# A spectral token mixer followed by an ELU feed-forward: the first two quads of the feed-forward with the plain eight block products, and the opening ordered anew

## The chip, the cores and the metric

The kernel runs on one NeuronCore of one Trainium2 chip, and the figure is the device time of one execution in microseconds. All arithmetic is in float32. Lower is better.

## The reference

```python
X = np.fft.rfft(x, axis=1)                      # x: (8, 3008, 256)
Y = X * (filt_r + 1j * filt_i)[None]            # filters: (1505, 256)
y = np.fft.irfft(Y, n=3008, axis=1)
t = y.reshape(24064, 256)
h = t @ w_in                                    # w_in: (256, 2048)
g = np.where(h > 0, h, np.exp(np.minimum(h, 0)) - 1)
out = (g @ w_out).astype(np.float32)            # w_out: (2048, 256)
```

The feed-forward's weights come as float64: the kernel converts each of them on the chip from its two 32-bit words.

## The kernel before

**The feed-forward.** It is the bulk. The 8 batches b are cut into 6 groups of tokens m (448 tokens in m = 0, 512 in the others), and the 2048 hidden units into 4 parts q. A **quad** is one (b, m, q); there are 192, and TensorE goes through them one after another. In each quad both layers are 2 x 2 block matrices, multiplied with Winograd's seven products instead of eight: `up_steps` gives seven products per quad for the first layer, `down_steps` seven for the second, and the downs of quad i-1 stand between the ups of quad i in a pattern of U and D. A product is two matrix multiplications, and the profile shows it as four records of 128x224 or 128x256.

The seven products need sums: of the weights (`w_sums`, four additions for each half layer, kept as slices 4 to 6 of `w_in[q]`, `w_out[q]` and in place in slice 1), of the tokens (`n_sums`, and in the first group four subtractions at the end of `n_first`), of the hidden units (four subtractions in the tail of `up_steps`) and of the results (seven additions, in `down_steps`' tail, `c_unit` and `c_last`). ScalarE copies products out of PSUM and does Relu and Exp of the ELU; VectorE joins the products and does the ELU's maximum.

**The order.** The kernel writes each engine's instructions in the order in which they are to run (`tc.manual_schedule`): engines take them in order, and a wait holds up all that stands behind it on that engine. Work that is not a product is placed by hand: `at(quad, place, fn, ...)` puts a step at one of five places in a quad (2, 4, 0, 3, 1 in order of time), and the list `early` holds the weights' and the first batches' steps of quads 0 to 9. Items 2 to 5 of the quads are (0, 1, 0..3), and the rest of group (0, 0) comes as items 6 and 7. So (0, 0) is summed in two parts: the result of its first two quads is kept in `part` and added by `c_part` in quad 9.

**The opening.** Before quad 0 batch 0 goes through the mixer on its own path: `x_load_first`, `a_first` (six of them), `t_first`, and for eight groups of frequencies `b_first`, `products` (four VectorE multiplications each, two sets per group) and `bi_first`, then `y_write_first`, `y_read_first` and `n_first`. Nine `warm` multiplications stand between the last `bi_first` and `n_first`. Weights are fetched in 16 pieces k (`w_fetch`, from SP's queue), and each is converted by `w_split` (VectorE, two instructions), `w_float` (ScalarE, three), `w_join` (VectorE, two) and `w_mult` (VectorE or GpSimd); pieces 0, 1 are `w_in[0]`, 2, 3 `w_out[0]`, 4, 5 `w_in[1]`, 6, 7 `w_out[1]`, and so on. `OPEN` places these among the groups. From quad 2 on, `a_unit`, `b_unit`, `bi_unit` and `n_unit` carry the mixer of batches 1 to 7 between the products; `x_unit` (VectorE or, by `XPOOL`, GpSimd) prepares their input.

Of the kernel before, what the change touches and what calls it, by code (L numbers as in the profile page):

```python
# [37 lines left out]
XPOOL = ((1, 1), (0, 0), (0, 1), (0, 1), (1, 1), (0, 0))  # L38
WTMP = (0, 1, 0, 1, 0, 2, 3, 1, 0, 3, 3, 2, 3, 2, 3, 2)
# [107 lines left out]
def kernel(  # L147
# [338 lines left out]
    def b_unit(b, g):  # L486
# [96 lines left out]
    def half(m):  # L583

        return 224 if m == 0 else 256
# [23 lines left out]
    def n_first(w):  # L609

        h = half(0)
        (y0, y1, s) = ysets[0]
# [10 lines left out]
        b11, b12, b21, b22 = b1[:, 0], b1[:, 1], b2[:, 0], b2[:, 1]  # L623
        t1, t2, t4 = (s[:, i, 0:h] for i in range(3))
# [109 lines left out]

    PLACE = {1: (0, 0), 5: (0, 1), 3: (1, 0), 7: (1, 1), 2: (2, 0), 6: (2, 1), 4: (3, 0)}

    def down_steps(b, m, q):
        h = half(m)
        g = g_of.pop((b, m, q))
        begin, last = q == 0 or (b, m, q) == (0, 0, 2), q == 3 or (b, m, q) == (0, 0, 1)  # L740
# [16 lines left out]
        def tail():  # L757
# [4 lines left out]
            if q == 1:  # L762
                c = part
            else:
                c = kp.tile([P, 2, 512], FP32, tag="c", name="c")
# [155 lines left out]
    with tc.manual_schedule():  # L921


        with tc.tile_pool(name="boot", bufs=1) as bp:
# [22 lines left out]
            for k in range(4):  # L947
                nc.tensor.matmul(warm, t2[:, 0, 0, 0:P], t2[:, 0, 0:2].rearrange("p u d -> p (u d)"), start=True, stop=True)
# [6 lines left out]
            x_load_first(1)  # L955
            nc.sync.dma_start(once, once_d)
            nc.sync.dma_start(gs[:, 1:3], gs_d[:, 1:3])
            x_load_first(0)
            x_load_first(2)
            x_load_first(3)  # L960
            x_load_first(5)
# [21 lines left out]
            f_read_first(2, 4, 0, nc.sync)  # L983
            f_read_first(2, 4, 1, nc.gpsimd)
# [6 lines left out]
            OPEN = {4: ((w_split, 1),),  # L991
                    6: ((w_float, 1, 1),),
                    7: ((tn_read, 0, 1), (w_split, 0), (w_float, 1, 2),),
                    8: ((w_float, 0, 1), (w_float, 1, 0),),
                    9: ((w_float, 0, 0), (w_join, 0, 1), (w_join, 1, 0, 1), (w_mult, 1, nc.vector),),
                    10: ((w_fetch, 3, nc.sync), (w_float, 0, 2),),
                    11: ((w_join, 0, 0), (w_mult, 0, nc.vector), (w_fetch, 5, nc.sync),),
                    12: ((w_split, 2), (w_float, 2, 0, 1), (w_join, 2, 1), (w_fetch, 4, nc.sync), (w_float, 2, 2), (w_join, 2, 0),),
                    13: ((w_mult, 2, nc.gpsimd), (w_split, 4), (w_split, 3), (w_sums, 1, nc.gpsimd),),
                    14: ((w_fetch, 6, nc.sync), (w_float, 3, 1),),  # L1000
                    15: ((w_fetch, 7, nc.sync), (w_float, 4, 1), (w_float, 3, 0),),
                    16: ((w_float, 3, 2), (w_float, 4, 0), (w_join, 3, 0), (w_join, 4, 1),),
                    17: ((w_split, 6), (w_float, 6, 0), (w_join, 6, 1), (w_float, 6, 1, 2), (w_float, 4, 2), (w_join, 3, 1), (w_join, 6, 0), (w_mult, 6, nc.gpsimd), (w_fetch, 9, nc.sync), (w_split, 5), (w_split, 9), (w_join, 4, 0),),
                    18: ((w_float, 5, 0), (w_fetch, 8, nc.sync), (w_mult, 3, nc.vector), (w_join, 5, 1), (w_float, 5, 1), (w_split, 7), (w_float, 9, 1),),
                    19: ((w_float, 5, 2), (y_write_first, 4, 8, 24), (w_mult, 4, nc.gpsimd),)}
# [6 lines left out]
            a_first(0)  # L1012
            a_first(1)
            conv(1)
            conv(2)
            a_first(2)
            conv(3)
            conv(4)
            a_first(3)
            conv(5)  # L1020
            a_first(4)
            conv(6)
            a_first(5)
# [41 lines left out]
        def at(quad, place, fn, *a):  # L1065
# [3 lines left out]
        early = ((0, 2, w_sums, 3, nc.gpsimd), (0, 2, y_read, 0, 1), (0, 2, w_fetch, 11, nc.sync), (0, 2, y_write_first, 0, 8, 24), (0, 2, w_float, 7, 0), (0, 2, w_join, 5, 0), (0, 2, x_load, 1, 1), (0, 2, w_float, 9, 0),  # L1069
                 (0, 4, w_float, 7, 1), (0, 4, w_split, 8), (0, 4, w_join, 7, 1), (0, 4, w_float, 7, 2),  # L1070
                 (0, 0, w_join, 7, 0),
                 (0, 3, w_fetch, 10, nc.sync), (0, 3, w_mult, 7, nc.gpsimd), (0, 3, w_mult, 5, nc.gpsimd), (0, 3, y_write_first, 2, 8, 24), (0, 3, w_fetch, 12, nc.sync), (0, 3, x_load, 1, 0), (0, 3, w_float, 8, 1),
                 (0, 1, w_float, 8, 2), (0, 1, w_sums, 5, nc.gpsimd), (0, 1, y_write_first, 6, 8, 24), (0, 1, y_write_first, 3, 8, 24),
                 (1, 2, w_float, 8, 0), (1, 2, w_split, 11), (1, 2, x_unit, 1, 0, 0),
                 (1, 4, n_unit, 0, 1), (1, 4, w_fetch, 15, nc.sync), (1, 4, w_float, 9, 2),
                 (1, 0, y_write_first, 5, 8, 24), (1, 0, x_unit, 1, 1, 0), (1, 0, w_join, 9, 1), (1, 0, x_unit, 1, 1, 1), (1, 0, w_sums, 7, nc.gpsimd), (1, 0, n_sums, 0, 1, 0, 1), (1, 0, w_join, 8, 1),
                 (1, 3, w_float, 11, 0), (1, 3, n_sums, 0, 1, 2), (1, 3, w_float, 11, 1),
                 (1, 1, w_join, 8, 0), (1, 1, w_mult, 8, nc.gpsimd),
                 (2, 4, w_float, 11, 2), (2, 4, w_join, 9, 0), (2, 4, w_join, 11, 0), (2, 4, w_mult, 9, nc.gpsimd),
                 (2, 0, x_unit, 1, 0, 1), (2, 0, w_sums, 9, nc.gpsimd), (2, 0, w_fetch, 14, nc.sync),  # L1080
                 (2, 3, w_split, 10), (2, 3, w_float, 10, 0),
                 (2, 1, w_float, 10, 1, 2), (2, 1, w_join, 10, 0), (2, 1, w_join, 11, 1), (2, 1, x_load, 1, 3), (2, 1, x_load, 1, 2), (2, 1, f_arrange, 1, 1),
                 (3, 2, c_unit, 0, 0),
                 (3, 4, x_unit, 1, 2, 0), (3, 4, w_fetch, 13, nc.sync), (3, 4, w_mult, 11, nc.gpsimd), (3, 4, w_join, 10, 1), (3, 4, x_unit, 1, 3, 0),
                 (3, 0, w_mult, 10, nc.gpsimd), (3, 0, x_unit, 1, 3, 1), (3, 0, w_split, 12),
                 (3, 3, f_arrange, 0, 0), (3, 3, w_float, 12, 1), (3, 3, y_write_first, 1, 8, 24),
                 (3, 1, x_unit, 1, 2, 1),
                 (4, 2, w_float, 12, 2), (4, 2, y_write_first, 7, 8, 24), (4, 2, w_split, 13), (4, 2, f_arrange, 0, 1), (4, 2, w_float, 12, 0),
                 (4, 4, w_float, 13, 1), (4, 4, w_join, 12, 1), (4, 4, x_unit, 1, 4, 0), (4, 4, w_float, 13, 0), (4, 4, x_unit, 1, 5, 0), (4, 4, w_float, 13, 2),
                 (4, 0, w_join, 13, 1), (4, 0, x_unit, 1, 5, 1), (4, 0, f_arrange, 1, 0), (4, 0, x_unit, 1, 4, 1), (4, 0, w_join, 13, 0), (4, 0, w_join, 12, 0), (4, 0, tn_read, 0, 2),  # L1090
                 (4, 3, y_read, 0, 2), (4, 3, w_mult, 12, nc.gpsimd),
                 (4, 1, w_mult, 13, nc.gpsimd), (4, 1, w_sums, 11, nc.gpsimd), (4, 1, w_sums, 13, nc.gpsimd), (4, 1, w_split, 14),
                 (5, 2, w_split, 15),
                 (5, 4, c_last, 0, 0), (5, 4, w_float, 14, 0), (5, 4, w_float, 15, 0), (5, 4, w_float, 14, 1), (5, 4, w_float, 15, 1), (5, 4, w_join, 15, 1), (5, 4, w_float, 14, 2), (5, 4, w_float, 15, 2),
                 (5, 0, w_join, 14, 1), (5, 0, w_join, 15, 0),
                 (5, 3, w_join, 14, 0), (5, 3, w_mult, 15, nc.gpsimd), (5, 3, w_mult, 14, nc.vector),
                 (5, 1, w_sums, 15, nc.gpsimd),
                 (6, 2, n_unit, 0, 2), (6, 2, y_read, 0, 3),
                 (6, 0, n_sums, 0, 2, 0, 1), (6, 0, tn_read, 0, 3),
                 (7, 2, n_sums, 0, 2, 2),  # L1100
# [60 lines left out]
        items = [(b, m, q) for b in range(B) for m in range(6) for q in range(4)]  # L1161
        items[2:8] = items[4:8] + items[2:4]
        for i in range(-PER, len(items) + 3):
            ups, up_tail = up_steps(*items[i]) if 0 <= i < len(items) else ((), None)
            downs, down_tail = down_steps(*items[i - 1]) if 1 <= i <= len(items) else ((), None)
            ups, downs = list(ups), list(downs)
            for n, k in enumerate("DUUDUDDU" if i in opens else "UUDUDDU"):
# [53 lines left out]
```

## Time and profile before

| | us |
|---|---|
| median of 3 runs (2542.19 to 2544.31) | 2542.7 |
| profiled execution, own time | 2540.18 |
| its span in the profile | 2538.1 |
| TensorE busy (share of the span) | 2513.2 (99%) |
| VectorE busy | 2106.5 (83%) |
| ScalarE busy | 1528.9 (60%) |
| GpSimd busy | 158.1 (6%) |
| mean granted TensorE clock | 0.998 |

The span begins with the first instruction and ends with the last; the own time has some 2 us around it. Times of single steps below are counted from the span's start. Matrix multiplications are pipelined, so neighbouring records overlap, and a record is longer than the distance to the next.

### The profile page before, as it was taken

What the parts mean: (1) busy time and instruction counts of PE and PEld (TensorE: products, weight loads), DVE (VectorE), ACT (ScalarE), POOL (GpSimd) and SP (SyncE); (2) the same over time, 40 slices, a digit from 0 to 9 for tenths busy, and PEclk for the clock granted to TensorE, in tenths of its full rate; (3) what the DMA queues carried; (4) which work ended last, traced back from release to release, by engine and by line L of the source; (5) the groups of instructions that cost most, each with busy time, mean ns of one, the idle gap of its engine ahead of it and who ended that gap; (6) DMA issues with size and microseconds to landing.
All of it is one profiled execution on the core that took longest, in us unless ns stands there. A gap on an engine that the chain in (4) does not pass through costs nothing.

```text
span 2538.1 us, 43881 instructions
## 1 busy us (share of the span) xinstructions
PE 2513.2 (99%) x16748; PEld 2140.8 (84%) x16748; DVE 2106.5 (83%) x3667; ACT 1528.9 (60%) x2706; POOL 158.1 (6%) x229
## 2 busy tenths in 40 slices
PE   9999999999999999999999999999999999999998
PEld 5787789888898888888889888888889888898887
DVE  6998998888988889798887888878887788866766
ACT  6665666655566555656566656666555565555554
POOL 3531000000000000000000000000000010000000
PEclk9999999999999999999999999999999999999999
DMA  7744445323243322433234322333223032220010
GB/s 207 204 112 100 104 99 130 76 58 90 60 99 80 70 65 55 104 65 78 63 82 112 69 58 59 74 84 71 57 47 84 21 69 50 54 46 18 13 24 17
DMA packets 224929, 192.08 MB, mean 76 GB/s; under 512 B 125221, under 2 KB 205639, under 8 KB 221983
## 3 DMA queue, kind: packets, MB, share of 16 engines
q1 hardware_dynamic: 213791, 165.44, 27.7%
q0 software_dynamic: 9776, 23.58, 4.6%
q8 instruction: 132, 2.16, 0.4%
q14 instruction: 78, 0.64, 0.1%
q10 hardware_dynamic: 1152, 0.26, 0.1%
HBM read 117.33 MB, written 74.97 MB: 76 GB/s over the span
## 4 chain that ended last, share of the span: by engine, by line
PE 93%; DVE 3%; DMA 1%; SPq 1%; ACT 1%; issue 1%; DVEq 0%; ACTq 0%
PE po L750 44%; PE phs L667 25%; PE phd L667 12%; PE pha L667 6%; PE pso L595 2%; PE pv L560 1%; PE pf L494 1%; PE psa L296 1%; PE pse L595 0%; DMA xc<-in_x_dram 0%; DVE g L675 0%; DMA x<-in_x_dram 0%; DVE g L689 0%; SPq L816 0%; PE po L381 0%
## 5 line engine op out<-in xcount | busy, mean ns | idle before, releaser
L750 PE MATMUL po<-g,wo 128*128 128x256 f32 (+1 forms) x5376 | 1316.3, 377 | 0.0
L750 PEld LDWEIGHTS po<-g,wo 128*128 128x128 f32 x5376 | 1013.9, 190 | 169.9 <-issue 50.6
L678 ACT ACTIVATE g<-phs 128x512 f32<-128x512 f32 (+1 forms) x576 | 339.1, 589 | 686.3 <-PE phs L667 685.8
L667 PE MATMUL phs<-y,wi 128*128 128x256 f32 (+1 forms) x2288 | 580.9, 376 | 2.4 <-ACT g L678 1.4
L685 ACT ACTIVATE e<-e 128x512 f32<-128x512 f32 (+1 forms) x768 | 477.2, 621 | 24.3
L667 PEld LDWEIGHTS phs<-y,wi 128*128 128x128 f32 x2288 | 429.4, 190 | 60.3 <-ACT g L678 3.9
L675 DVE TENSOR_TENSOR g<-phd,g 128x512 f32<-128x512 f32 (+1 forms) x384 | 258.2, 672 | 231.6 <-ACT e L685 141.3
L684 ACT ACTIVATE e<-g 128x512 f32<-128x512 f32 (+1 forms) x576 | 353.3, 613 | 68.0 <-DVE g L675 57.3
L689 DVE SCALAR_TENSOR_TENSOR g<-e,g 128x512 f32<-128x512 f32 (+1 forms) x576 | 392.6, 682 | 0.8 <-ACT e L685 0.7
L689 DVE SCALAR_TENSOR_TENSOR g<-e,phs 128x512 f32<-128x512 f32 (+1 forms) x192 | 129.7, 676 | 116.0 <-ACT e L685 115.7
L667 PE MATMUL phs<-ys,wi 128*128 128x256 f32 (+1 forms) x784 | 200.2, 378 | 5.7 <-ACT g L678 2.6
L667 PE MATMUL phd<-y,wi 128*128 128x256 f32 (+1 forms) x768 | 195.6, 377 | 4.2 <-DVE g L675 4.2
L667 PE MATMUL phd<-ys,wi 128*128 128x256 f32 (+1 forms) x768 | 194.0, 375 | 0.8 <-DVE g L675 0.7
L667 PE MATMUL pha<-ys,wi 128*128 128x256 f32 (+1 forms) x752 | 190.0, 375 | 0.0
L684 ACT ACTIVATE e<-phs 128x512 f32<-128x512 f32 (+1 forms) x192 | 113.0, 588 | 114.2 <-PE phs L667 113.6
L667 PEld LDWEIGHTS phs<-ys,wi 128*128 128x128 f32 x784 | 147.4, 191 | 24.2 <-POOL wi L904 2.2
L667 PEld LDWEIGHTS phd<-y,wi 128*128 128x128 f32 x768 | 145.1, 191 | 24.1 <-DVE g L675 7.6
L667 PEld LDWEIGHTS phd<-ys,wi 128*128 128x128 f32 x768 | 145.7, 190 | 18.1 <-DVE g L675 1.8
L667 PEld LDWEIGHTS pha<-ys,wi 128*128 128x128 f32 x752 | 142.9, 190 | 16.4
L675 DVE TENSOR_TENSOR g<-pha,g 128x512 f32<-128x512 f32 (+1 forms) x192 | 129.0, 672 | 19.1 <-PE pha L667 15.8
L726 DVE TENSOR_TENSOR g<-g,g 128x512 f32<-128x512 f32 (+1 forms) x192 | 131.9, 687 | 6.7
L729 DVE TENSOR_TENSOR g<-g,g 128x512 f32<-128x512 f32 (+1 forms) x192 | 131.1, 683 | 6.7
(210 smaller groups left out, 2081.5 us busy)
## 6 DMA issues: line engine op xcount, KB each, us to landing
t<-yd SPq DMA_DIRECT2D x94, 256.0 KB
fall<-fp POOLq DMA_DIRECT2D x112, 192.0 KB, 5.2
t<-z SPq DMA_DIRECT2D x112, 192.0 KB
yd<-t SPq DMA_DIRECT2D x112, 192.0 KB
out_dram<-o SPq DMA_DIRECT2D x632, 32.0 KB
xc<-in_x_dram SPq DMA_DIRECT2D x153, 128.0 KB
z<-t SPq DMA_DIRECT2D x144, 128.0 KB
tn<-tn_t SPq DMA_DIRECT2D x47, 128.0 KB
```

The lines of the kernel that those rows point to most:

```text
L296: nc.tensor.matmul(p[32 * o:32 * o + 32, :, :], w[r, ts(o, 32)], x_part(t, o % 2, o // 2)[r], start=True, stop=True, tile_position=(32 * a ...
L494: nc.tensor.matmul(pf[p][1][32 * a:32 * a + 32, js, :], fb[r, v, :], t2[r, js, a, :], start=True, stop=True, tile_position=(32 * p, 32 * a))
L595: nc.tensor.matmul(p[o:o + 64, dh, ds(64 * q, n)], t[r, i - 4 * m, ds(dh * P + o, 64)], w[r, i - 4 * m, 0:n], start=True, stop=True)
L667: nc.tensor.matmul(ps[:, a, 0:h], w_in[q][:, COMBO[n], a, :], y[n], start=start and a == 0, stop=True, skip_group_check=True)
L675: nc.vector.tensor_tensor(out=g[o], in0=i0, in1=i1, op=ALU.add)
L678: nc.scalar.activation(out=g[o], in_=i0, func=AXT.Copy)
L684: nc.scalar.activation(out=e, in_=src, func=AXT.Relu, scale=-1.0)
L685: nc.scalar.activation(out=e, in_=e, func=AXT.Exp, scale=-1.0)
L689: nc.vector.scalar_tensor_tensor(out=g[n], in0=es[n], scalar=1.0, in1=src, op0=ALU.subtract, op1=ALU.max)
L726: nc.vector.tensor_tensor(out=b12, in0=b22, in1=b12, op=ALU.subtract)
L729: nc.vector.tensor_tensor(out=g["t4"], in0=g["b21"], in1=g["t2"], op=ALU.subtract)
L750: nc.tensor.matmul(po[i][:, u, 0:h], w_out[q][:, COMBO[n], a, :], g[n][:, a, :], start=begin and a == 0 and n in (1, 3, 6, 4), stop=True, ...
```

## The change

Quads 0 and 1, which are (0, 0, 0) and (0, 0, 1), take eight block products in each layer, straight from the blocks of weights and tokens, with the ELU read from PSUM. Their hidden units need no sums, their results no joining: two ScalarE copies put them in `part`. So the sums of `w_in[0]`, `w_out[0]`, `w_in[1]`, `w_out[1]` are first needed in quads 2 to 4, and the token sums of group (0, 0) (`n_rest`) in quad 6. Steps of the opening and of quads 0 to 9 are placed anew: fetches, conversions, which engine does a `w_mult`, `w_sums` or `x_unit` (GpSimd does fewer of each), and the loads and steps of batches 1 and 2. In `b_unit` of the groups other than 0, the four multiplications of row part 3 come after the twelve others. One of the four first `warm` multiplications goes, and `a_first(5)` comes before `a_first(4)`.

```diff
-XPOOL = ((1, 1), (0, 0), (0, 1), (0, 1), (1, 1), (0, 0))
-WTMP = (0, 1, 0, 1, 0, 2, 3, 1, 0, 3, 3, 2, 3, 2, 3, 2)
+XPOOL = ((0, 0), (1, 1), (0, 0), (0, 1), (0, 0), (0, 0))
+WTMP = (0, 1, 0, 1, 0, 2, 3, 1, 0, 3, 3, 2, 3, 0, 0, 3)
...
+        else:
+            both.sort(key=lambda w: w[1] == 3)
...
-        b11, b12, b21, b22 = b1[:, 0], b1[:, 1], b2[:, 0], b2[:, 1]
-        t1, t2, t4 = (s[:, i, 0:h] for i in range(3))
+        ys[0, 0] = (b1[:, 0], b1[:, 1]), (b2[:, 0], b2[:, 1])
+
+    def n_rest():
+        (b11, b12), (b21, b22) = ys[0, 0]
+        t1, t2, t4 = (ysets[0][2][:, i, 0:half(0)] for i in range(3))
...
+    def up_plain(q):
...
+        def mm(i, j, k):
+            if k == 0:
+                held[i, j] = bank("phw")
+            ps = held[i, j][1]
+            for a in range(2):
+                nc.tensor.matmul(ps[:, a, 0:h], w_in[q][:, 2 * k + i, a, :], y[k][j],
+                                 start=k == 0 and a == 0, stop=True, skip_group_check=True)
+            if k == 1:
+                e = es[i, j] = ep.tile([P, 2, 256], FP32, tag="e", name="e")[:, :, 0:h]
+                nc.scalar.activation(out=e, in_=ps[:, :, 0:h], func=AXT.Relu, scale=-1.0)
+                nc.scalar.activation(out=e, in_=e, func=AXT.Exp, scale=-1.0)
+
+        def top(i, j):
+            n, ps = held.pop((i, j))
+            nc.vector.scalar_tensor_tensor(out=g[i][:, j], in0=es[i, j], scalar=1.0, in1=ps[:, :, 0:h],
+                                           op0=ALU.subtract, op1=ALU.max)
+            banks.append(n)
...
+        return [first] + [(lambda w=w: then(*w)) for w in (
+            (1, 0, 0), (1, 0, 1, 0, 0), (0, 1, 0), (0, 1, 1, 1, 0), (1, 1, 0), (1, 1, 1, 0, 1))], tail
+
+    def down_plain(q):
...
+            for i, j, k in products:
+                for a in range(2):
+                    nc.tensor.matmul(po[i][:, j, 0:h], w_out[q][:, 2 * k + i, a, :], g[k][:, j, a, :],
+                                     start=q == j == k == a == 0, stop=True, skip_group_check=True)
+
+        def end():
+            step((1, 1, 1))
+            if q == 1:
+                for i in range(2):
+                    nc.scalar.activation(out=part[:, i, 0:2 * h].rearrange("p (u h) -> p u h", u=2),
+                                         in_=po[i][:, :, 0:h], func=AXT.Copy)
...
-            for k in range(4):
+            for k in range(3):
                 nc.tensor.matmul(warm, ...
...
-            f_read_first(0, 2, 1, nc.gpsimd)
             w_fetch(1, nc.sync)
             w_fetch(0, nc.sync)
             f_read_first(0, 2, 0, nc.sync)
+            f_read_first(2, 4, 0, nc.sync)
+            f_read_first(0, 2, 1, nc.gpsimd)
+            f_read_first(2, 4, 1, nc.gpsimd)
             w_fetch(2, nc.sync)
...
+                    19: ((w_join, 4, 0), (x_load, 1, 0), (w_float, 5, 2), (w_fetch, 8, nc.sync), (y_write_first, 4, 8, 24),)}
+            AORD = (0, 1, 2, 3, 5, 4)
...
+        early = ((0, 2, y_read, 0, 1), (0, 2, w_fetch, 11, nc.sync), (0, 2, y_write_first, 0, 8, 24),
+                 (0, 4, x_load, 1, 1), (0, 4, w_float, 7, 0, 1), (0, 4, w_join, 5, 0),
+                 (0, 0, y_write_first, 2, 8, 24), (0, 0, w_mult, 4, nc.vector), (0, 0, w_float, 9, 0), (0, 0, w_join, 7, 1), (0, 0, w_float, 7, 2),
...
+                 (1, 4, y_write_first, 5, 8, 24), (1, 4, w_sums, 1, nc.vector), (1, 4, n_unit, 0, 1), (1, 4, w_float, 8, 1),
...
+                ups, up_tail = up_plain(i) if i < 2 else up_steps(*items[i])
...
+                downs, down_tail = down_plain(i - 1) if i < 3 else down_steps(*items[i - 1])
```

The first `x_load` of batch 2 moves from quad 11, place 0, to quad 9, place 3; its first `x_unit` stays at quad 11, place 1.

More of the change, by code (lines that the diff above doesn't have):

```diff
@@ L611, in n_first @@
         h = half(0)
-        (y0, y1, s) = ysets[0]
+        (y0, y1, _) = ysets[0]
         b1, b2 = y0[:, :, 0:h], y1[:, :, 0:h]
@@ L732, in up_steps, with first, then, tail @@
         return (s1, s2, s6, s5, s7, s3, s4), tail
+    def up_plain(q):
+        h = half(0)
+        y = ys[0, 0]
+        g = [gps[q % 2].tile([P, 2, 2, 256], FP32, tag=tag, name=tag)[:, :, :, 0:h] for tag in ("g1", "g2")]
+        held, es = {}, {}
+        def mm(i, j, k):
[14 more added lines that the diff above has]
+            banks.append(n)
+        def first():
+            mm(0, 0, 0)
+            mm(0, 0, 1)
+        def then(i, j, k, *before):
+            mm(i, j, k)
+            if before:
+                top(*before)
+        def tail():
+            top(1, 1)
+            g_of[0, 0, q] = g
+        return [first] + [(lambda w=w: then(*w)) for w in (
+            (1, 0, 0), (1, 0, 1, 0, 0), (0, 1, 0), (0, 1, 1, 1, 0), (1, 1, 0), (1, 1, 1, 0, 1))], tail
@@ new lines, in down_plain, with step, tail @@
+    def down_plain(q):
+        h = half(0)
+        g = g_of.pop((0, 0, q))
+        if q == 0:
+            po_of[0, 0] = [psO.tile([P, 2, 256], FP32, tag="po%d" % i, name="po%d" % i) for i in range(2)]
+        po = po_of[0, 0]
+        def step(*products):
+            for i, j, k in products:
[8 more added lines that the diff above has]
+                                         in_=po[i][:, :, 0:h], func=AXT.Copy)
+        def tail():
+            pass
+        return [lambda: step((0, 0, 0), (1, 0, 0))] + [(lambda w=w: step(w)) for w in (
+            (0, 0, 1), (1, 0, 1), (0, 1, 0), (1, 1, 0), (0, 1, 1))] + [end], tail
@@ L739, in down_steps @@
         g = g_of.pop((b, m, q))
-        begin, last = q == 0 or (b, m, q) == (0, 0, 2), q == 3 or (b, m, q) == (0, 0, 1)
+        begin, last = q == 0 or (b, m, q) == (0, 0, 2), q == 3
         if begin:
@@ L761, in tail @@
             p35, p7 = (k[1][:, u, 0:h] for u in range(2))
[L762 to L765, printed above, removed]
+            c = kp.tile([P, 2, 512], FP32, tag="c", name="c")
             (c11, c12), (c21, c22) = ((c[:, i, 0:h], c[:, i, h:2 * h]) for i in range(2))
@@ L955 @@
             x_load_first(1)
+            nc.sync.dma_start(gs[:, 1:3], gs_d[:, 1:3])
             nc.sync.dma_start(once, once_d)
-            nc.sync.dma_start(gs[:, 1:3], gs_d[:, 1:3])
             x_load_first(0)
+            x_load_first(5)
             x_load_first(2)
             x_load_first(3)
-            x_load_first(5)
             x_load_first(4)
@@ L989, in conv @@
                     fn(*a)
[L991 to L1005, printed above, removed]
@@ L1011 @@
             conv(0)
-            a_first(0)
-            a_first(1)
+            AORD = (0, 1, 2, 3, 5, 4)
+            a_first(AORD[0])
+            a_first(AORD[1])
             conv(1)
             conv(2)
-            a_first(2)
+            a_first(AORD[2])
             conv(3)
             conv(4)
-            a_first(3)
+            a_first(AORD[3])
             conv(5)
-            a_first(4)
+            a_first(AORD[4])
             conv(6)
-            a_first(5)
+            a_first(AORD[5])
             conv(7)
@@ L1066, in at @@
             plan.setdefault((quad, place), []).append((fn, a))
[L1069 to L1096, printed above, removed]
@@ L1129 @@
                         at(t + s, 1, z_write, b, c)
-                for g, steps in zip(range(0, NG, 2), (((1, 4), (1, 1), (2, 0), (2, 3), (1, 1), (3, 4), (3, 3), (3, 1)), ((1, 2), (2, 0), (3, 2), (1, 4), (2, 0), (2, 3), (3, 0), (3, 1)), ((1, 2), (2, 2), (2, 2), (1, 4), (1, 1), (1, 1), (3, 4), (3, 1)), ((1, 4), (2, 4), (2, 4), (2, 2), (2, 2), (2, 4), (2, 1), (3, 1))) if b == 1 else STEPS):
+                for g, steps in zip(range(0, NG, 2), (((1, 4), (2, 2), (2, 0), (2, 3), (1, 1), (3, 0), (3, 3), (3, 1)), ((0, 1), (2, 4), (3, 2), (1, 0), (2, 2), (2, 0), (3, 2), (3, 1)), ((0, 1), (2, 4), (2, 0), (1, 2), (1, 1), (1, 1), (3, 3), (3, 1)), ((1, 4), (2, 4), (2, 4), (2, 4), (2, 0), (2, 0), (2, 1), (3, 1))) if b == 1 else STEPS):
                     s = t + ((6, 10, 14, 18) if b == 1 else GQ)[g // 2]
@@ L1163 @@
         for i in range(-PER, len(items) + 3):
-            ups, up_tail = up_steps(*items[i]) if 0 <= i < len(items) else ((), None)
-            downs, down_tail = down_steps(*items[i - 1]) if 1 <= i <= len(items) else ((), None)
+            ups = downs = ()
+            up_tail = down_tail = None
+            if 0 <= i < len(items):
+                ups, up_tail = up_plain(i) if i < 2 else up_steps(*items[i])
+            if 1 <= i <= len(items):
+                downs, down_tail = down_plain(i - 1) if i < 3 else down_steps(*items[i - 1])
             ups, downs = list(ups), list(downs)
```

45 lines of the change are left out of this document (40 added, 5 removed).

## The prediction

> **What bounds the kernel.** I read the engines' shares on the page first, then the busy times by stretch, then TensorE's waits and the order in time of TensorE and VectorE in the stretches that have gaps.
>
> ```profile
> PE 2513.2 (99%) x16748; PEld 2140.8 (84%) x16748; DVE 2106.5 (83%) x3667; ACT 1528.9 (60%) x2706; POOL 158.1 (6%) x229
> ```
>
> TensorE (PE) is the bound, and a share of 99% says that little can be won unless products go away, which this change does not do. The question is where the missing 25 us lie. By stretch (start:end, length, busy time and records of PE, weight loads, DVE, ACT, POOL, then PE's granted clock, DMA share, GB/s):
>
> ```profile
> 65.94:71.29 5.35, 2.82 (x14) 1.98 (x13) 5.21 (x9) 3.22 (x7) 2.87 (x4) 1.00 0.93 262
> 71.29:76.29 5.00, 5.00 (x16) 4.44 (x17) 3.29 (x6) 3.57 (x7) 2.82 (x4) 0.66 0.77 249
> 76.29:80.65 4.36, 2.43 (x13) 2.11 (x13) 4.12 (x6) 4.30 (x9) 3.85 (x5) 1.00 0.80 237
> 80.65:85.83 5.18, 5.18 (x77) 4.67 (x78) 5.14 (x11) 2.61 (x5) 0.00 (x0) 0.67 0.88 221
> 92.23:151.46 59.23, 55.06 (x321) 45.49 (x321) 55.56 (x79) 42.39 (x75) 34.19 (x33) 1.00 0.76 214
> 151.46:260.00 108.54, 104.09 (x769) 88.42 (x783) 99.84 (x176) 64.59 (x116) 11.23 (x16) 1.00 0.32 68
> 260.00:2500.00 2240.00, 2240.00 (x14978) 1926.81 (x14947) 1859.18 (x3254) 1344.29 (x2372) 72.87 (x120) 1.00 0.30 68
> ```
>
> From 260 us on PE has no gap in 2240 us. So the end moves exactly as the opening moves, and only the first 260 us need working out. In them PE idles and, after two of the idle stretches, runs at 0.66 of its clock. Its waits from 55 to 270 us (waiting line, releaser, total, times, longest):
>
> ```profile
> PE phd L667 <- DVE g L675: 5.0, 5, 2.7
> PE phs L667 <- ACT g L678: 4.0, 3, 1.9
> PE phs L667 <- DVE ys L627: 1.9, 1, 1.9
> PE phs L667 <- POOL wi L902: 1.3, 1, 1.3
> PE phs L667 <- ACT t L302: 1.0, 1, 1.0
> ```
>
> These are sums: of tokens (`ys`), of weights (L902), of hidden units (`g`). In time, quad 0 begins at 65.94, quad 1 at 76.29, quad 2 at 92.23:
>
> ```profile
> 65.94 0.98 PE L667 MATMUL phs<-y,wi 128*128 128x224 f32 x4
> ...
> 69.66 1.00 PE L667 MATMUL phs<-ys,wi 128*128 128x224 f32 x4 [1.90 <-DVE ys L627]
> ...
> 76.29 0.92 PE L667 MATMUL phs<-y,wi 128*128 128x224 f32 x4
> ...
> 92.23 1.03 PE L667 MATMUL phs<-y,wi 128*128 128x256 f32 x4
> ```
>
> A product is four such records. Undisturbed ones stand 0.755 us apart at 224 columns (76.29 to 77.05) and 0.865 us at 256.
>
> **The change, part by part**, from the order of each engine's instructions in the changed kernel as built, with durations from this trace.
>
> *A. Up to quad 0.* VectorE's 32 products of the mixer run from 25.94 to 55.32: 32 x 0.60 = 19.2 us, and 14 conversion instructions among them take the other 10.1 (three splits at 0.95 instead of 0.34 while GpSimd runs, and 1.0 of waits for ScalarE). Now 17 stand among them, but eight are splits: 8 x 0.34 + 6 x 0.60 + 0.7 + 0.8 = 7.8, and 0.7 for waits: 8.5. All that follows (last `bi_first`, its write, its read back, `n_first`) is one chain and moves by 10.1 - 8.5 = **-1.6**. Bounds: -2.5 without waits, +0.5 if three splits and both waits are as slow as before. The dropped warm multiplication, the order of `a_first` and of the first loads I cost at nothing: the first VectorE product waits for the filter's transfers until 25.94, and PE was ready at 25.4. If the x pieces, 512 KB each at 220 GB/s or 2.3 us apart, came late, 0.5 us of cover would go first. Piece 2's fetch, moved behind the filter's second part, is not needed before its split some 17 us later.
>
> *B. Quads 0 and 1.* From 65.94 to 92.23 PE did 21 products and `n_unit` in 26.29 us. Now it does 24 (eight ups twice, eight downs once) before quad 2 begins: 24 x 0.755 = 18.1, and 1.1 for `n_unit` (153.93 to 155.02) = 19.2. Nothing in quad 0 waits for a sum. What could make it wait, counted from the first product: ScalarE does Relu and Exp of two blocks, four conversion steps (2.5 us), then two more blocks, so the second block's bank is free at 6.4 and the last two at 8.4 and 9.5; PE wants them at 8.2 and, for `n_unit`, at 10.7. `w_in[1]`: piece 4 is multiplied on VectorE behind the first block's maximum at 5.3, piece 5 on GpSimd at 5.9; PE wants them at 6.0 and 6.8. Quad 1's `g1` lies where the transfer `y_write_first(0)` still reads; SP now has `x_load(1, 0)` and two more steps ahead of it and gets it out by about 9 after the first product, so it lands at 11 to 13, where 12 is wanted. SP's 50 issues from here took 27.3 us before; their 6.4 MB fit 25.6 at the 250 GB/s of 122 to 151 us. I put 1.0 for these: 20.2, so **-6.1**. The saving is 4.5 us of idle time and 3.4 of clock (0.34 x 5.00 + 0.33 x 5.18) and the small gaps around them, less 2.3 for three extra sets of products. Bounds: -7.1 with no wait, -2 if each of the five links is late by one.
>
> *C. Quads 2 to 5*, 59.23 us with 4.17 idle. The fourth set of extra products costs 0.755. VectorE is the engine to watch, busy for 55.56. Between the first maximum chain of quad 2 and that of quad 5 it now has 67 instructions, before 59 (46.6 us): five of the result's additions are gone, but four token sums of `n_rest`, four of `w_mult`, three of `x_unit` and two of conversions have come. Alone, 53 of 0.60 and 14 of 0.34 are 36.6. GpSimd's share was 59 instructions that would be 32.2 alone taking 45: half of its 24.5 busy us are lost to VectorE. Now GpSimd has about 17, so 36.6 + 8.5 = 45.1, against PE's 42.5 for these quads. That leaves VectorE a little late again, but it starts level with PE instead of 2.5 us behind. In quad 5 GpSimd's sums of piece 13 are no longer behind a second multiplication. I take idle time of 1.9 instead of 4.2: -2.3 + 0.8 = **-1.5**; bounds -3.4 and +5, the latter if VectorE's mean stays at 0.79.
>
> *D. Quad 6 to 260 us*: 4.45 idle, of which 2.65 is one wait at 243.86. VectorE stands before it at `x_unit`:
>
> ```profile
> 236.70 0.69 DVE L269 TENSOR_TENSOR sd<-xc 128x512 f32<-128x512 f32 x1 [2.39 <-DMA t<-z]
> 238.31 0.69 DVE L269 TENSOR_TENSOR sd<-xc 128x512 f32<-128x512 f32 x1 [0.92 <-DMA xc<-in_x_dram]
> ```
>
> Its load was issued from 225.10 to 229.06, behind 24 output writes (11.4 us of SP). Now it is issued two quads earlier, ahead of those writes, which nobody waits for: **-2.5**. The other waits (0.73, 0.50, 0.57) may stay. Bounds -4.4 and +2, since steps of batch 1 are placed anew here.
>
> *E. After 260 us.* The row part put last: the sixteen multiplications of L494 all begin between 216.8 and 217.1 and run together (16 counted at once in every tenth from 217.0 to 217.3), so their order costs nothing. Nor did a `b_unit` wait for a transfer, so nothing is gained. 0; +0.1 each if the last four come in late, 21 x 0.1 = 2.
>
> Sum: -1.6 - 6.1 - 1.5 - 2.5 = -11.7. On the profiled execution's 2540.2 that is 2528.5. It ran 2.5 below the median, so for the median I take 2542.7 - 11.7 = **2531.0**.
>
> **The rivals.**
>
> *VectorE becomes the bound (slower).* Nine more `w_mult`, `w_sums` and `x_unit` steps are VectorE's instead of GpSimd's, and all steps stand in one queue with the ELU. From the first block's maximum (67.0) to quad 5's first addition there are 102 instructions; before, quad 5's was at 143.2. At a mean of (143.2 - 67.0)/102 = 0.75 us nothing is left of B and C, and above it the kernel loses. 0.82, a little over the 0.79 of 96.6 to 143.2, gives +7.5: 2550. For it: VectorE is 94% busy in C. Against: alone they mean 0.53 (53.8 us), and GpSimd, which makes the difference, has less to do.
>
> [...] An ELU maximum with both inputs in SBUF, 0.68 us elsewhere, took 1.63 at 100.46 while GpSimd's L264 ran from 100.27. [...]
>
> *The transfers are the limit (same).* 18.8 MB went out between 65.94 and 151.46 (12.7 MB in the last 59 us); at 250 GB/s they need 75 us of the 85. The quads can thus be at most 10 us ahead of them; if what stands in order behind x, weights and `y` takes most of that back, 6 to 8 us of B to D go, and 2538 to 2539 is left. Against: `b_unit` at 164.26 came 14 us after its last read was issued.
>
> *The gaps stay and only the products count (same).* If quads 0 and 1 wait for weights and transfers as they did for sums, A and D are -4.1, the extra products +3.0: 2541.6.
>
> **How the numbers follow.** What a measurement can tell from no change is 0.2%, 5.1 us: faster is below 2537.6, slower above 2547.8. The forecast (all bounds together reach 2525.3) has 0.76, transfers 0.08 and unchanged gaps 0.05, VectorE 0.11. The range goes from 2525.5 to 2540.5: it holds the forecast with B to D at half their worth and the transfers' case. Faster 0.76, same 0.13, slower 0.11.
>
> **What would show it.** A right: `n_first` near 62.6. B: the first eight products follow each other at 0.755, quad 2 begins near 84.5, no clock under 1.00 after 64. C: quad 6 begins near 142 instead of 151.46, VectorE's mean below 0.70 in quads 2 to 4. D: no wait of VectorE for xc near 230. E: L494 at 1.2 us per unit, no PE gap after 250. Wrong: VectorE over 97% busy with PE waiting for it in quads 2 to 5, or waits of PE or VectorE for transfers of over 5 us in all.

## The result and the profile after

The changed kernel takes 2535.8 us (median of 8, 2533.1 to 2539.2), the kernel before beside it 2542.05: a ratio of 0.9976 [0.9965, 0.9987], 6.2 us less, where 11.7 were forecast. The interval leaves out 1, so it is faster, by a quarter of a percent. The profiled execution took 2535.84 us with a span of 2534.0.

```profile
PE 2513.0 (99%) x16762; PEld 2142.1 (85%) x16762; DVE 2099.5 (83%) x3663; ACT 1524.3 (60%) x2700; POOL 140.8 (6%) x212
```

By stretch, in the columns of the table of before:

```profile
31.00:36.50 5.50, 5.00 (x32) 3.41 (x32) 4.26 (x7) 2.37 (x5) 1.15 (x3) 0.69 0.96 222
69.35:78.50 9.15, 9.15 (x48) 9.15 (x49) 5.82 (x10) 7.51 (x14) 2.11 (x2) 1.00 0.74 209
78.50:88.96 10.46, 10.46 (x115) 9.98 (x114) 9.40 (x19) 5.87 (x11) 3.40 (x3) 1.00 0.77 214
88.96:123.51 34.55, 30.05 (x186) 24.45 (x184) 34.17 (x47) 23.14 (x41) 20.62 (x22) 1.00 0.80 223
88.96:150.81 61.85, 56.85 (x326) 46.35 (x325) 58.93 (x87) 44.01 (x77) 29.60 (x33) 1.00 0.82 226
150.81:256.00 105.19, 103.56 (x769) 88.41 (x783) 99.67 (x176) 64.14 (x116) 11.22 (x16) 1.00 0.38 87
256.00:2500.00 2244.00, 2243.78 (x14997) 1930.19 (x14970) 1864.27 (x3262) 1344.92 (x2375) 72.56 (x120) 1.00 0.30 67
```

Quads 0 and 1 (69.35 to 88.96) are the success: TensorE has no gap in them and keeps its full clock, 19.61 us where it took 26.29. But they begin 3.4 us later than before, not 1.6 earlier, and quads 2 to 5 take 61.85 us instead of 59.23, with VectorE busy for 34.17 of the first 34.55. TensorE's waits from 20 to 270 us:

```profile
PE phd L672 <- DVE g L680: 5.6, 6, 2.0
PE po L428 <- ACT tf L382: 1.3, 1, 1.3
PE phw L752 <- ACT y L623: 1.0, 1, 1.0
PE phs L672 <- ACT t L302: 0.7, 1, 0.7
```

The waits for sums of tokens and weights are gone, and with them the 2.65 us at 243.86. Left are a hidden block's sum on VectorE (L680), a ScalarE copy of batch 1's first transform (L302) and, new, two ScalarE copies in the opening (L382, L623).

**The late opening.** ScalarE, then VectorE and TensorE in order of time:

```profile
29.73 0.72 ACT L938 ACTIVATE wme<-wme,edges 128x512 f32<-128x512 uint32 x1 [2.67 <-DVE wme L929]
30.36 0.61 ACT L938 ACTIVATE wfl<-wm 128x512 f32<-128x512 uint32 x1
30.88 0.58 ACT L382 ACTIVATE tf<-po 112x512 f32<-112x512 f32 x1
```
```profile
29.27 0.42 DVE L929 TENSOR_SCALAR wme<-fall 128x512 uint32<-128x512 uint32 x1
...
38.56 0.69 DVE L946 SCALAR_TENSOR_TENSOR wme<-fall,wme 128x512 uint32<-128x512 uint32 x1 [2.29 <-ACT wme L938]
```
```profile
31.50 0.43 PE L428 MATMUL po<-rq,gs 48*64 48x256 f32 x1 [1.25 <-ACT tf L382]
```

The split of piece 1 (L929) stands behind the mixer's first products. ScalarE's conversions wait for it, and `t_first`'s copy `tf` waits behind them. TensorE then idles for 1.25 us, is granted half its clock from 32.76 to 36.17 (a dip, from here on; the mean of 31.0 to 36.5 is 0.69), and through ScalarE that comes back to VectorE as 2.29 us. Just before quad 0 it happens again: ScalarE stands at 67.02 before a conversion whose split waited for GpSimd, and `n_first`'s copies come behind three of them, at 68.78.

**VectorE in quad 3** (first fence), with GpSimd (second):

```profile
114.78 3.26 DVE L929 TENSOR_SCALAR rq<-wo 128x512 uint32<-128x512 uint32 x1
117.96 0.67 DVE L680 TENSOR_TENSOR g<-phd,g 128x512 f32<-128x512 f32 x1
```
```profile
114.53 1.45 POOL L264 TENSOR_TENSOR xc<-xc 128x512 f32<-128x512 f32 x1
115.93 1.83 POOL L1249 MEMSET fall<- 128x1024 f32 x2
```

A split that takes 0.42 us elsewhere took 3.26, from GpSimd's subtraction to the end of its two clearings (memory set to zero), and the sum behind it is the one TensorE waits for at 118.69 (1.97 us).

### The profile page after: what moved, and what is told of

Read it like the earlier page. It is cut to its first block, busy times and chain, and to the rows that moved or that the text cites. A ratio compares the mean times of both kernels' runs of the same rounds, so it can differ in the third digit from the quotient of the medians.

```text
span 2534.0 us, 43885 instructions
## 1 busy us (share of the span) xinstructions
PE 2513.0 (99%) x16762; PEld 2142.1 (85%) x16762; DVE 2099.5 (83%) x3663; ACT 1524.3 (60%) x2700; POOL 140.8 (6%) x212
## 4 chain that ended last, share of the span: by engine, by line
PE 93%; DVE 3%; ACT 1%; issue 1%; DMA 0%; SPq 0%; DVEq 0%; ACTq 0%
PE po L823 44%; PE phs L672 25%; PE phd L672 12%; PE pha L672 6%; PE pso L597 2%; PE pf L496 1%; PE pv L562 1%; PE psa L296 1%; PE pse L597 0%; DVE g L680 0%; DVE g L694 0%; DMA t4f<-in_moe_w_in_dram 0%; DVE c L839 0%; ACT rq L938 0%; DMA z<-t 0%
## 5 line engine op out<-in xcount | busy, mean ns | idle before, releaser
L823 PEld LDWEIGHTS po<-g,wo 128*128 128x128 f32 x5320 | 1002.7, 190 | 169.6 <-issue 50.2
L680 DVE TENSOR_TENSOR g<-phd,g 128x512 f32<-128x512 f32 (+1 forms) x380 | 256.0, 674 | 228.0 <-ACT e L690 140.6
L694 DVE SCALAR_TENSOR_TENSOR g<-e,g 128x512 f32<-128x512 f32 (+1 forms) x570 | 387.0, 679 | 0.7 <-ACT e L690 0.5
L680 DVE TENSOR_TENSOR g<-pha,g 128x512 f32<-128x512 f32 (+1 forms) x190 | 127.8, 673 | 19.6 <-PE pha L672 16.5
```

What stands on the lines that cost most here:

```text
L680: nc.vector.tensor_tensor(out=g[o], in0=i0, in1=i1, op=ALU.add)
L694: nc.vector.scalar_tensor_tensor(out=g[n], in0=es[n], scalar=1.0, in1=src, op0=ALU.subtract, op1=ALU.max)
L823: nc.tensor.matmul(po[i][:, u, 0:h], w_out[q][:, COMBO[n], a, :], g[n][:, a, :], start=begin and a == 0 and n in (1, 3, 6, 4), stop=True, ...
```

## The experiments

Each experiment ran 5 to 11 times in five rounds, and its ratio is to the kernel before timed beside it (medians of 2541.74 to 2542.34). The marks are of the one profiled execution each (us), and differ between executions of the same instructions (see a_split). B runs from the first product of quad 0 to quad 2, C from there to quad 6, and "rest" from quad 6 to the span's end.

| kernel | median | ratio to before | first product | B | C | rest |
|---|---|---|---|---|---|---|
| before | 2542.05 | | 65.94 | 26.29 | 59.23 | 2386.6 |
| changed | 2535.8 | 0.9976 [0.9965, 0.9987] | 69.35 | 19.61 | 61.85 | 2383.2 |
| a_split | 2535.1 | 0.9975 [0.9965, 0.9985] | 65.32 | 19.77 | 63.73 | 2383.5 |
| a_y_ahead | 2534.8 | 0.9975 [0.9965, 0.9985] | 65.92 | 20.69 | 60.93 | 2384.8 |
| c_order | 2534.9 | 0.9974 [0.9965, 0.9983] | 67.44 | 20.57 | 61.09 | 2384.3 |
| c_no_sums | 2532.7 | 0.9960 [0.9947, 0.9972] | 67.19 | 21.36 | 58.39 | 2383.8 |
| c_mult_back | 2540.5 | 0.9993 [0.9985, 1.0002] | 67.27 | 20.16 | 67.87 | 2384.5 |
| b_alone | 2544.0 | 1.0007 [0.9998, 1.0015] | 66.46 | 27.34 | 60.33 | 2387.9 |
| b_sums_off | 2539.6 | 0.9988 [0.9979, 0.9997] | 65.17 | 24.38 | 62.11 | 2386.9 |
| d_load_back | 2539.6 | 0.9992 [0.9983, 1.0002] | 69.06 | 19.82 | 63.26 | 2387.2 |
| e_order_back | 2536.8 | 0.9979 [0.9970, 0.9988] | 70.19 | 20.08 | 60.91 | 2384.2 |
| best1 | 2532.0 | 0.9958 [0.9945, 0.9972] | 65.71 | 20.09 | 61.10 | 2383.8 |
| best2 | 2530.3 | 0.9953 [0.9940, 0.9965] | 64.69 | 20.72 | 59.39 | 2383.2 |
| best3 | 2530.4 | 0.9953 [0.9940, 0.9965] | 65.99 | 20.20 | 59.32 | 2383.7 |

**a_split.** Piece 1 is split ahead of the first products.

```diff
-OPEN = {6: ((w_split, 0),),
+OPEN = {6: ((w_split, 0), (w_split, 1)),
...
-        8: ((w_split, 1), (w_float, 1, 1), (w_float, 0, 0),),
+        8: ((w_float, 1, 1), (w_float, 0, 0),),
```

> The changed kernel with one step moved: VectorE splits weight piece 1 ahead of the mixer's first four products instead of behind them. Theory one (order on ScalarE): in the changed kernel ScalarE's conversion of piece 1 stood at 29.73 us waiting for that split, and behind it the copy `tf` for which TensorE idled 1.25 us, then ran at half clock from 32.7 to 36 us and set back ScalarE and, by 2.29 us at 38.56, VectorE. Then that idle time, the clock dip and the long wait go, the first product of quad 0 comes at 66.3 to 67.0 us instead of 69.35, and the kernel takes about 2533.2 us (2.6 less than 2535.8). Theory two (the filter's transfers): the second VectorE product waited 1.00 us for the filter at 27.14, and everything else follows that; then the first product stays at 68.9 or later and the time within 0.5 us of 2535.8.

Measured: the idle time and the dip in the opening are gone, and so is VectorE's wait for ScalarE but for 1.21 us; `n_first` comes at 62.44 and the first product at 65.32. That is theory one's mechanism, and a little more. Its time is missed: 2535.1 cannot be told from the changed kernel. In this profile quads 2 to 5 took 1.9 us longer, because here the wait of 1.97 us in quad 3 was followed by half clock:

```profile
116.00:119.60 3.60, 3.60 (x23) 2.12 (x25) 3.50 (x5) 3.54 (x6) 1.88 (x3) 0.58 0.53 139
```

The gain of 4 us over the changed kernel's profile is more than the order's. Five other experiments have the changed kernel's opening whole, and in all of them TensorE idles for 1.03 to 1.34 us there. In three (c_order, c_no_sums, c_mult_back) no dip follows, and the first product comes at 67.19 to 67.44; in two (d_load_back, e_order_back) one does, as in the changed kernel, and it comes at 69.06 to 70.19. So the order without the dip is worth about 2 us, and the dip, which came in three of six executions, 1.6 to 3 more. Why the median fell by only 0.7 us, this one profile can't tell.

**a_y_ahead.** Piece 5 is split before piece 9, and a conversion of piece 9 comes behind `n_first`'s copies.

```diff
-(w_fetch, 9, nc.sync), (w_split, 9), (w_split, 5),),
+(w_fetch, 9, nc.sync), (w_split, 5), (w_split, 9),),
-(w_split, 7), (w_float, 9, 1),),
-19: ((w_join, 4, 0),
+(w_split, 7),),
+19: ((w_float, 9, 1), (w_join, 4, 0),
```

> The changed kernel with two conversion steps moved: piece 5 is split ahead of piece 9, and ScalarE's first conversion of piece 9 comes behind the copies of the first `y`. Theory: the first product waits 0.98 us for `y`, which ScalarE copied at 68.78, behind three conversions that had waited for GpSimd through the split of piece 9; with them out of the way the copies start at 67.6, the first product comes at 68.2 us instead of 69.35, and the kernel takes 1.1 us less, 2534.7. Rival: what is earlier here is taken back by quad 1's weights or by VectorE in quads 2 and 3, so the first product is earlier but quad 2 begins at 88.9 as before or quad 6 at 150.8 as before, and the time stays 2535.8.

Measured: the copies wait for TensorE alone, and the first product follows `n_first` by 1.73 us instead of 2.87. It gained 1.0 in the median, as expected in size, though that too is within the spread. Its first product at 65.92 is not a gain of 3.4 us: this execution had no dip, and against the three others without one it is 1.3 to 1.5 earlier.

**c_order.** Two splits go behind the sum that TensorE waits for.

```diff
-(2, 0, w_split, 10), (2, 0, w_float, 10, 0),
+(2, 3, w_split, 10), (2, 3, w_float, 10, 0),
-(3, 0, x_unit, 1, 3, 0), (3, 0, w_split, 12),
+(3, 0, x_unit, 1, 3, 0),
-(3, 3, x_unit, 1, 3, 1), (3, 3, w_float, 12, 1),
+(3, 3, x_unit, 1, 3, 1), (3, 3, w_split, 12), (3, 3, w_float, 12, 1),
```

> The changed kernel with two splits of weight pieces (10 and 12, with their first conversion) moved on VectorE behind the third hidden block's sum and maxima of quads 2 and 3. Theory one (order): TensorE's two waits of 1.81 us at 100.64 and 1.97 us at 118.69 are for a sum that stood behind these splits (1.49 + 0.94 and 0.95 + 3.26 us on VectorE); both go, quad 6 begins at 147 to 148 us instead of 150.81 and the kernel takes 3 us less, about 2532.8. Theory two (amount): VectorE was busy for 34.17 of the 34.55 us of quads 2 and 3, so the same work in another order moves the waits to other products; quads 2 to 5 still take 61 to 62 us and the time stays within 1 us of 2535.8.

Measured: both waits go, but C stays at 61.09; the unchanged order took 60.91 and 60.93 in e_order_back and a_y_ahead. Part of the time appears again as 1.53 us before `a_unit` at 118.69, behind the split that was moved. Theory two held: the amount of time that VectorE spends, not this order, decides there.

**c_no_sums.** `w_fill`, one ScalarE copy of a half layer's slices 0 to 2 to its slices 4 to 6, takes the place of GpSimd's sums of pieces 5, 7, 9 and 11, which this kernel leaves out of the computation.

```diff
-(2, 4, w_sums, 5, nc.gpsimd),
+(2, 4, w_fill, 5),
...
-(2, 3, w_sums, 9, nc.gpsimd),
+(2, 3, w_fill, 9),
```

> The changed kernel without GpSimd's weight sums of pieces 5, 7, 9 and 11 (16 instructions; ScalarE writes copies in their place, one each, so those sums are left out of the computation). VectorE's own instructions are the same and in the same order. Theory one (contention): in quads 2 and 3 VectorE was busy for 99% of the time, but 9 us of it were instructions that took 0.95 to 3.26 us instead of 0.34 or 0.60 while GpSimd had one running; without these 16 the most of that goes, quads 2 to 5 take 57 to 59 us instead of 61.85 and the kernel 3 to 4 us less than 2535.8, about 2532. Theory two (VectorE has too many instructions of its own there, 87 against 79): quads 2 to 5 still take 61 us or more and the time stays within 1 us of 2535.8.

```profile
88.55:146.94 58.39, 56.59 (x325) 46.41 (x325) 53.25 (x87) 46.22 (x81) 16.54 (x17) 1.00 0.86 241
```

Measured: theory one. VectorE does the same 87 instructions in 53.25 busy us instead of 58.93. What its instructions took beyond their 0.42 or 0.69 us elsewhere, summed from the order in time, is 5.4 us where the changed kernel has 11.2. About 1 us of the 3.5 by which C is shorter is chance: in this execution the split of quad 3 did not meet the clearings (1.49 us instead of 3.26). In a_y_ahead and e_order_back, where it did not either, C is 60.93 and 60.91.

**c_mult_back.**

```diff
-(2, 4, w_mult, 9, nc.vector),
+(2, 4, w_mult, 9, nc.gpsimd),
-(2, 1, w_mult, 11, nc.vector),
+(2, 1, w_mult, 11, nc.gpsimd),
-(4, 3, w_mult, 12, nc.vector),
+(4, 3, w_mult, 12, nc.gpsimd),
```

> The changed kernel with the multiplications of weight pieces 9, 11 and 12 on GpSimd again, as before. Theory one (contention): VectorE loses four instructions of 0.34 to 0.60 us (1.9 us), but GpSimd runs some 5 us more, and of GpSimd's 29.9 busy us in quads 2 to 5 VectorE lost 11.2, so 1.9 us come back as slower instructions; quads 2 to 5 take 61 to 63 us and the time stays within 1 us of 2535.8. Theory two (the steps given to VectorE made it the bound, the prediction's rival): quads 2 to 5 take 60 us or less and the kernel 1.5 to 2 us less, 2534.

Measured: neither. It is 4.7 us slower than the changed kernel, and C takes 67.87 us, at a mean clock of 0.95:

```profile
99.44 1.11 PE L672 MATMUL phd<-y,wi 128*128 128x256 f32 x3 [2.13 <-DVE g L680]
...
120.30 1.05 PE L672 MATMUL phd<-y,wi 128*128 128x256 f32 x2 [3.10 <-DVE g L680]
```

GpSimd's 35.3 busy us cost VectorE 12.9 instead of 11.2, the sum came later, and half clock followed both waits. In quad 5 TensorE also waited 1.0 us for weights that GpSimd had multiplied and summed. These three of the steps given to VectorE were thus worth taking; for them the prediction's rival, which blamed such steps, is refuted. The others were not tried.

**b_alone and b_sums_off.** b_alone is the kernel before with `up_plain`, `down_plain` and `n_rest` of the changed one. There the weight sums stand where they were, and the plain products read slice 1 after a sum has replaced it. b_sums_off also moves `w_sums` of pieces 1, 3, 5, 7 and 9 to the changed kernel's places and engines.

> The kernel before with only the plain quads 0 and 1 and the token sums put off; order of the opening, weight sums, loads and row parts as before. Theory (term B): the first product comes at 66 us as before, quad 2 begins 19.6 to 21 us after it instead of 26.29, with no clock dip between; quads 2 to 5 take 59 to 62 us, the wait at 243.86 stays, and the kernel takes 2542 - 6 + 1 to 2 = 2537 to 2538. Rival: VectorE and GpSimd bound quads 2 to 5, so what quads 0 and 1 save is taken back there: those take 64 us or more and the kernel 2541 to 2542.

> The kernel before with the plain quads 0 and 1, the token sums put off and the weight sums of pieces 1, 3, 5, 7 and 9 put off to quads 1 to 3, as in the changed kernel; order of the opening, loads, multiplications and row parts as before. b_alone, where the weight sums stood where they were (so that the plain products read a sum in place of one weight block), took 27.3 us from the first product to quad 2, with 5 us of waits for GpSimd's weights and half clock behind them. Theory (term B is the putting off of the sums, not the plain form): quad 2 now begins 19.6 to 21.5 us after the first product. What is put off falls into quads 2 to 5 with GpSimd's other work: they take 60 to 63 us, and the kernel 2542.3 - 6 + 2.5 = 2538 to 2539.5. Rival (the quads wait for the weight pieces themselves, whatever becomes of the sums): quad 2 begins 24 us or more after the first product and the kernel takes 2542 or more.

```profile
PE phw L750 <- POOL wi L957: 2.8, 1, 2.8
PE phw L750 <- POOL wi L972: 2.2, 1, 2.2
```

These are b_alone's waits. The plain quads by themselves gain nothing: they wait for GpSimd's multiplication of piece 5 (L957) and for the sums (L972). With the sums put off the second wait goes and B falls by 3.0; the first stays, 2.83 us at 75.12 with half clock behind it, and B is 24.38, so the rival of b_sums_off was right about B and wrong about the time. GpSimd in b_sums_off:

```profile
72.43 1.41 POOL L963 TENSOR_TENSOR wo<-wfl,wme 128x256 f32<-128x256 f32 x2 [8.28 <-DVE wme L944]
73.80 1.27 POOL L957 TENSOR_TENSOR wi<-zq 128x512 f32<-128x512 f32 x1
```

Piece 5 (`zq`) had been joined by 67.25, but its multiplication stands behind that of piece 7 (`wo`), which waited 8.28 us. The changed kernel multiplies piece 7 on VectorE, later, and piece 5's multiplication is done 5.96 us after the first product instead of 9.90. The wait of 2.83 us and the 1.7 us that the dip costs are nearly all of the 4.8 us of B that were left. That is read from the traces; moving piece 7 alone was not tried. So B was won by several parts together: the plain form alone gained nothing.

**d_load_back.** One place: `(((-15, 3), ((-13, 1)` becomes `(((-13, 0), ((-13, 1)`.

> The changed kernel with the load of batch 2's first x piece back at its old place, two quads later, behind the output writes. Theory (term D): VectorE's sum of that piece near 230 us waits for the load again, TensorE waits about 2.65 us behind it near 241, and the kernel takes 2.5 us more, about 2538.3. Rival: the steps around it were moved too and give it slack, so the load is in time and nothing changes (2535.8, within 0.5).

```profile
243.87 0.70 PE L672 MATMUL phd<-y,wi 128*128 128x256 f32 x2 [1.97 <-DVE g L680]
```

Measured: the wait is back, with VectorE waiting 1.01 and 0.40 us for the load at 236 to 237 us, and the time is 3.8 us higher. Half clock followed TensorE's wait: 1.97 and 1.7 us make up most of it.

**e_order_back.** The `else: both.sort(...)` is left out.

> The changed kernel without the sort that puts a group's fourth row part last. Theory (term E): the sixteen multiplications of a unit run together whatever their order, nothing changes, 2535.8 within 0.5. Rival: the sort saved 0.1 us in each of 31 units, and the kernel takes 3 us more, 2538.9.

Measured: 1.0 us more, with ranges that overlap (2535.5 to 2540.1). From the first `b_unit` after 260 us to the last it took 1897.0 us against 1896.2, and 1896.4 in the kernel before, which has no sort either. Its opening had a dip of twice the usual length. The sort may be worth up to 1 us, not 3; this stays open.

**best1, best2, best3.** best1 joins the three edits. best2 adds the first line below, best3 the rest.

```diff
-            at(4, 0, nc.gpsimd.memset, fbufs[i], 0.0)
+            at(4, 1, nc.gpsimd.memset, fbufs[i], 0.0)
...
-(2, 1, w_float, 10, 1, 2), (2, 1, w_join, 10, 0),
+(3, 2, w_float, 10, 1, 2), (3, 2, w_join, 10, 0),
```

> The changed kernel with all three edits of a_split, a_y_ahead and c_order together. Theory one (VectorE bounds quads 2 to 5): the first product comes at about 64 us and quad 2 begins at 83.7, but a_split alone lost 1.8 of the 4 us it had gained in its profile again by quad 6, so quad 6 begins at 147 and the kernel takes about 2533.5. Theory two (the gains add, as order alone decides): quad 6 begins at 144.5 and the kernel takes 2530.5 to 2531.5.

> best1 with GpSimd's two clearings of the filter's buffers (1.84 us) moved from quad 4's middle to its end, in GpSimd's order behind the sums of piece 13 and ahead of the filter's reads. In best1 VectorE's 0.34 us instruction at 112.85 took 2.13 us, as long as these clearings ran beside it (112.85 to 114.69), and in the changed kernel 3.26. Theory one (a clearing holds VectorE up like an addition does): that instruction takes 0.95 or less, TensorE's wait of 1.54 us at 116.48 goes, and the kernel takes 1.2 to 1.8 us less than best1's 2532.0, about 2530.5. Theory two (the delay is the two-input operations' alone, the clearings have no part in it): the instruction stays at 2 us or more, as GpSimd's sums of piece 11 move up into the same place, and the time stays within 0.5 us of 2532.0.

> best2 with two of ScalarE's conversions of piece 10 (1.46 us, at 100.01 in best1) and VectorE's step behind them moved from the end of quad 2 behind the copies of batch 1's first transform, for which TensorE waited 0.87 us at 102.01. Expected: that wait goes, quad 3 begins 0.9 us earlier, and the kernel takes 0.9 us less than best2. Rival: piece 10's later steps come late by as much, a wait of the same size appears in quad 4, and the time is that of best2.

best1 took 2532.0 us, between its two theories. Its first product came at 65.71, not at about 64, and its C is 61.10, so the order alone did nothing there. best2 is as expected. The same split in best1 (first fence, VectorE and GpSimd) and in best2 (second):

```profile
112.85 2.13 DVE L928 TENSOR_SCALAR rq<-wo 128x512 uint32<-128x512 uint32 x1
112.85 1.84 POOL L1249 MEMSET fall<- 128x1024 f32 x2
```
```profile
112.45 0.42 DVE L928 TENSOR_SCALAR rq<-wo 128x512 uint32<-128x512 uint32 x1
112.47 0.98 POOL L971 TENSOR_TENSOR wo<-wo 128x256 f32<-128x256 f32 x1
```

The wait before `a_unit` goes and C falls to 59.39. best3's wait at the start of quad 3 goes, and another of 0.58 us appears later in quad 3, at 111.61: much as its rival has it, with the time of best2. best2, at 2530.3, is 11.7 us faster than before (0.9953 [0.9940, 0.9965]) and beats both kernels.

## Why the prediction was right, and where it was not

**The bound and the sign** held: TensorE has no gap worth the name after 256 us, and the end moved as the opening did.

**A** failed: -1.6 forecast, +3.4 in the profile, beyond its bound of +0.5. The step is "and 0.7 for waits: 8.5". The conversions' instructions took some 8 us where it gave them 7.8, but VectorE waited 4.7 us among them (1.00, 0.64, 0.36, 2.29, 0.42). The dip has a part in that, and so chance: c_order, without one, waited 2.6 us (0.47, 1.69, 0.42), and openings of this order without a dip are 1.3 to 1.5 later than before. I looked at how many steps VectorE has and not at what ScalarE has queued behind each: a conversion in front of TensorE's copy. The second failed step is that all behind the last `bi_first` "moves by" the same amount, where `n_first`'s copies were 1.1 us late. With the split moved, `n_first` came at 62.44 in a_split, where 62.6 had been forecast, and at 62.96 to 64.18 in best1 to best3.

**B** was right: 19.61 against 20.2, no wait, no dip. Its condition that piece 5 be multiplied by 6.8 held, with 5.96; in b_sums_off it did not, and TensorE waited.

**C** had the wrong sign: +2.6 against -1.5. Of VectorE's 67 instructions, counted rightly, the stretch between the maxima took 48.8 us (93.90 to 142.66) against 45.1. The step is "Now GpSimd has about 17", that is busy us, half of which VectorE was to lose. That stretch in the kernel before (first) and the changed one (second), GpSimd's busy time before the clock:

```profile
96.60:143.19 46.59, 43.85 (x270) 35.73 (x269) 44.63 (x61) 32.34 (x58) 30.51 (x28) 1.00 0.77 225
93.90:142.66 48.76, 44.09 (x268) 35.47 (x267) 48.24 (x68) 31.38 (x56) 25.39 (x27) 1.00 0.82 230
```

GpSimd was busy for 25.4 us: the four weight sums of piece 7, put off by B, land here (4.0 us), and two clearings of 1.83 us together held VectorE up for as long as they ran (3.26 us for a split of 0.42). Before, it was 30.5 us, not the 24.5 of the prediction, so that VectorE lost 0.4 of them, not half. The rival's bound was real in quads 2 and 3, with VectorE 99% busy and TensorE waiting. The sign that I had named, over 97% in quads 2 to 5, was not reached over all four (95%). But VectorE's mean from 72.36 to 142.66 is 70.3/102 = 0.69 us, under the 0.75 that decided, and the cause was contention with GpSimd, as c_no_sums shows (53.25 busy us instead of 58.93 for the same 87 instructions), more than the count of steps. Chance has a part of about 1 us here too: in 3 of 7 executions with this order of split and clearings the two did not meet.

**D** was right: from quad 6 on the changed kernel is 3.4 us faster by the table (2386.6 - 2383.2), 1.8 to 3.4 over the kernels with the load moved; -2.5 was forecast.

**E**: rated 0; at most 1.

**The other rivals.** No wait for transfers of the size that the transfers' case needs appeared. Gaps that stay, priced at 2541.6, is the case that b_alone and b_sums_off (2544.0 and 2539.6) put on the chip.

In the sum A missed by 5.0 and C by 4.1, B, D and E gave 1.5 more than forecast: -11.7 became -4.1 in the profiles (2538.1 to 2534.0) and -6.2 in the medians. The time lies in the range because B and D came about as forecast and the range left room for half of what B to D were worth; the sum itself was half wrong, and two terms had the wrong sign. best2 reaches 2530.3 by four changes of order in the opening and quads 2 to 4, so 5.5 us more were to be had there; that this meets the 11.7 forecast is chance.

## What to carry to other kernels

Where engines run in a fixed order, price a moved step by what stands behind it in the queue of every engine that waits for it, not by its own length: a split 0.8 us long, put behind four products (28.94 us, where a_split has it at 21.93), cost TensorE 1.25 us in the changed kernel's profile, and 1.7 more by the dip behind it. Work put off does not vanish; count the engines' busy time in the stretch where it lands, clearings included. And look for short waits of the bound engine first, since each can cost twice, as this one did. A single profile can hold two or three us of chance (with the changed kernel's opening the first product came at 67.19 to 70.19): compare the marks of all executions that share the instructions.

## What the runs showed of the hardware

**Half clock came in portions.** Every dip that the profiles show up to 2500 us is 3.41 us at half clock or twice that (76.6 to 83.4 in b_alone, 31.7 to 38.5 in e_order_back), and so takes 1.7 us of work or 3.4; in the changed kernel it is the 0.31 x 5.50 = 1.7 of 31.0 to 36.5. The dips followed idle times of 1.25 to 3.1 us, but not each time: 1.97 us at 118.69 in the changed kernel had none behind it, nor had 2.65 at 243.86 before; 1.97 at 115.33 in a_split had one. best1 to best3, with no wait over 1.54 us, showed none. Nor is the length of the wait all: 1.25 us in d_load_back and 1.34 in e_order_back had a dip behind them, 1.33 in c_order had none. Why one wait brings half clock and another of its length does not, no run shows.

**A clearing on GpSimd held a split on VectorE up** for its whole length: 2.13 us for a split beside 1.84 us of clearing in best1, 0.42 without in best2. Whether they meet is partly chance: with the changed kernel's order the split took 3.25 or 3.26 us in four executions, and 1.49 in a_y_ahead and c_no_sums, where it was done first and the clearings took 2.12 us instead of 1.83; in e_order_back TensorE waited 0.19 us behind it, as in a_y_ahead (0.20), where the changed kernel waited 1.97. An addition was not held up by one, in the one case of the kernel before. Its clearings (first) ran from 125.16 to 127.00 beside the second of two additions, which took 0.69 us, the median of its line; GpSimd's subtraction ran from 123.62 to 125.22 beside the first, which took 1.75 us where the median is 0.68:

```profile
125.16 1.84 POOL L1175 MEMSET fall<- 128x1024 f32 x2
124.01 1.75 DVE L728 TENSOR_TENSOR g<-g,g 128x512 f32<-128x512 f32 x1
125.80 0.69 DVE L729 TENSOR_TENSOR g<-g,g 128x512 f32<-128x512 f32 x1
```

What makes a split wait for a clearing, where this addition did not, no trace shows.
